# Last stage of a fused linear-attention and GLU kernel: transposes one pair ahead, numerators in one piece, and a longer wait for x tiles

## The chip, the cores and the metric

The kernel runs on one core of a Trainium2 chip. Its engines work side by side, each through its own queue of instructions in a fixed order: TensorE (PE) multiplies matrices into eight PSUM banks, VectorE (DVE) and ScalarE (ACT) can read these banks, GpSimd (POOL) works on on-chip tiles only, and SyncE (SP) starts the transfers (DMA). An instruction that waits holds up everything behind it on its own engine. The metric is the time of one execution on the device, in microseconds.

## The reference, cut to what matters

```python
xn = layernorm(x)                                   # x: 2048 x 1024, f32
q, k, v = split(xn @ wqkv)                          # 32 heads of 32
phi(t) = concat(softmax(t @ w_phi), softmax(-(t @ w_phi)))
num = phi(q) @ (phi(k).T @ v);  den = phi(q) @ sum(phi(k)) + 1e-6
s = (num / den) @ wo
h = sigmoid(xn @ w_gate) * (xn @ w_up)              # 2048 x 3584
g = silu(h @ w_down)
out = x + s * g
```

## The kernel before, in words

Every large product is one level of a Strassen-like scheme: seven products (`B11, T2, T3, B21, T1, T4, B22`) of half-size blocks, summed in PSUM and by DVE. Each f32 operand is held as a high and a low part; `split` makes them (the high part by an ACT cast, L219, the low part by a DVE subtraction, L220), and `mm3` issues three matmuls (L224, L225, L226), 128 x 128 by 128 x 512 each. So one "product" in the text below is one `mm3`, three matmul instructions, unless an operation of the scheme is meant.

The stages follow each other on PE: projections, the GLU's first layer (in two chunks of rows, c = 0 and 1), its second layer (the "down" stage, L1279 and on), and the last stage, attention output times `wo`.

Beside the products, generator tasks do the rest of the work in small steps. While chunk 0 of the GLU runs, `x_task` prepares the eight row tiles of chunk 1: it loads a tile, normalises it (L269 to L284: statistics on DVE, a square root and the scaling on ACT), writes it to DRAM in another order (`xs_d`, four DMAs, L665) and reads it back (L667). After three `yield`s, each one step of the task, two DVE transposes (L672) put it in place; in the second tile of each couple `x_sums` adds eight POOL pieces (L79). POOL also makes the sums of the GLU weights (`glu_sums`) and the gate products `pool.mul` (L79 too) that let DVE reuse the buffers of `u1` and `u2` (L1185, L1188).

The last stage runs over eight pairs of row tiles (`tp_`, L1348). A pair is seven operations of four products (28 products, 84 matmuls): B11, T2, T3, B21, T1, T4, B22. Their sums read the banks: L1370 (T2), L1376 (T3), L1383 (B21), L1386 (T1, T4, B22); T4 adds into the bank of T3 and B22 into that of T1, so B22's first product waits until T1's sum has been read. Beside a pair the operands of the next one are made: eight DVE transposes of the weighted features (`phi_transpose`, L817: for each half of the heads hb, each tile u, each q; the second for a tile starts the DMA of the next features, L810, from `f_d`), then `numerators` (16 matmuls of 64 rows, L832, which the profile lists as 32 records), four ACT copies out of their banks (L837), and `o_operands`: four POOL sums of two pieces each and seven splits.

The order in which the code calls these is only the starting point: a scheduler reorders the instructions of each engine by its own estimate, unless `tc.issue_after(i)` holds a piece back behind instruction `i` in that estimate. `attend` gives the places in a pair: transposes at the products 1 to 4 and 8 to 11, numerators at product 13. Nothing anchors them in before.

Of the kernel before, what the change touches and what calls it, by code (L numbers as in the profile page):

```python
# [17 lines left out]
P = 128  # L18
# [120 lines left out]
def hedgehog_glu_kernel(  # L139
# [82 lines left out]
    def mm3(o, a, b, first, last, **kw):  # L222

        nc.tensor.matmul(o, a[0], b[0], start=first, stop=False, **kw)  # L224
        nc.tensor.matmul(o, a[0], b[1], start=False, stop=False, **kw)  # L225
        nc.tensor.matmul(o, a[1], b[0], start=False, stop=last, **kw)  # L226

# [430 lines left out]
    def x_task(t):  # L658
        th, u = t % CTT // 4, t % 4
        xt, dst = x_load(t, 52), halves(53 + th)  # L660
        yield
        yield from norm_steps([t], [xt])
        yield
        for n in range(4):
            nc.sync.dma_start(xs_d[t - CTT, :, :, n].rearrange("q s c -> s q c"),  # L665
                              xt[n * DH:(n + 1) * DH].rearrange("s (q c) -> s q c", q=4))
        nc.sync.dma_start(xt, xs_d[t - CTT].rearrange("q s n c -> (q s) (n c)"))  # L667
        yield
        yield
        yield  # L670
        for q in range(2):
            nc.vector.transpose(dst[q].rearrange("p (k n s) -> p n k s", n=4, s=DH),  # L672
                                xt.rearrange("p (n k d) -> p n k d", n=4, d=DH)[:, :, 4 * q:4 * q + 4])
            i = {(0, 0): B11, (1, 0): B21, (1, 1): B22}.get((q, th))
            if i is not None:
                operand(1, i, u, dst[q])
        if th:
            x_sums(u, halves(53), halves(54))
# [134 lines left out]
    def phi_transpose(tp_, u, hb, q):  # L813
# [5 lines left out]
        if q:  # L819
            e_load(u)  # L820

    def numerators(tp_):

        sums = []
        for hb in range(2):
            for q in range(2):
                ps, ph = nmr.next(), units_ph[hb, q]
                kv = slots[KVB[hb]][:, q].rearrange("p (k m) -> p k m", m=P)
                for j in range(2):
                    for b in range(2):  # L830
                        bs = slice(b * 64, b * 64 + 64)
                        nc.tensor.matmul(ps[bs, j * 256:(j + 1) * 256], kv[:, 2 * j + b, bs], ph[:, 2 * j + b], start=True,  # L832
                                         stop=True, skip_group_check=True)
                sums.append((hb, q, ps))
        for hb, q, ps in sums:
            o = oraw[hb].rearrange("p u (g t) -> p u g t", t=P)
            nc.scalar.copy(o[:, :, 2 * q:2 * q + 2], ps.rearrange("p (j u t) -> p u j t", j=2, u=2))  # L837
            if q:
                o_operands(tp_, hb)
# [20 lines left out]

    def attend(tp_):

        turned = [(phi_transpose, tp_, u, hb, q) for hb in range(2) for u in range(2) for q in range(2)]
        return list(zip((1, 2, 3, 4, 8, 9, 10, 11, 13), turned + [(numerators, tp_)]))

# [198 lines left out]
    wd = [(5, lambda j=j: wd_sums(j, *(halves(47, 52) if j < WD1 else spare))) for j in range(NJ)]  # L1064
    xs = [(8, lambda t=t: x_task(t)) for t in (CTT + 4 * a + q for q in range(4) for a in range(2))]
    os = [(6, lambda k=k: o_task(k)) for k in range(4)]
# [169 lines left out]
    def evacuate(i, p):  # L1236
# [18 lines left out]
        else:  # L1255
            nc.vector.tensor_add(u1[p], u1[p], b)
            gate_out(u1[p], t, 1)
# [12 lines left out]
    for n, (i, j, cs) in enumerate(dsteps):  # L1270
        w, hs = dready[n]
        for c in cs:
            for u in range(4):
                p = 4 * c + u
                mm3(banks[p], cut(pair(hs[c]), slice(u * P, (u + 1) * P)), pair(w),
                    j == 0 and i in (B11, T2, T3, T1), j == NJ - 1, skip_group_check=True)
        wfree.append(w)
        hfree.extend(hs.values())
# [32 lines left out]
        if n == ND - NJ:  # L1311
            step(1000)
            side.extend([lambda fn=fn, a=a: behind_split(fn, *a) for _, (fn, *a) in attend(0)])
        if len(dready) == ND:
# [30 lines left out]
    for _ in range(2):  # L1345
        gx_load()
    abank = {}
    for tp_ in range(NTP):  # L1348
        nxt = attend(tp_ + 1) if tp_ + 1 < NTP else []
        n = 0  # L1350
# [5 lines left out]
        for i in range(7):  # L1356
# [4 lines left out]
            for k in range(4):  # L1361
                mm3(ps, (o[0][:, k], o[1][:, k]), pair(WO[i][k]), i in opening and k == 0, k == 3, skip_group_check=True)
                n += 1
                while nxt and nxt[0][0] <= n:
                    fn, *a = nxt.pop(0)[1]
                    fn(*a)
            if i == B11:
                nc.scalar.copy(u1, ps)
            elif i == T2:
                nc.vector.tensor_add(u1, u1, ps)  # L1370
                for r in (T4, B22) if last else ():
# [3 lines left out]
            elif i == T3:  # L1375
                nc.vector.tensor_add(u2, u1, ps)  # L1376
            else:
# [3 lines left out]
                if i == B21 or last and i != T1:  # L1381
                    y = {B21: y11, T4: y21, B22: u1}[i]
                    nc.vector.tensor_mul(y, g, ps)  # L1383
                else:
                    y = {T1: u2, T4: y21, B22: u1}[i]
                    nc.vector.tensor_add(y, u2 if i == T1 else u1, ps)  # L1386
                    eng.mul(y, y, g)
# [34 lines left out]
```

## Time and profile before

| what | value |
|---|---|
| time, median of 3 runs (lowest to highest) | 2351.07 us (2348.71 to 2352.66) |
| the profiled execution, and its span | 2350.23 us, 2348.5 us |
| PE busy | 2331.4 us, 99% of the span |
| DVE, POOL, ACT busy | 69%, 49%, 41% |
| DMA, share of 16 engines | 78% |

PE is busy nearly throughout, and its matmuls are pipelined: a row of 0.39 us does not mean that the next one starts 0.39 us later. How fast PE goes is read from the starts of consecutive matmuls. In the timeline a row gives start, duration, engine, line, operation, output and inputs, shape, count, and in brackets the idle time of the engine before it with what ended it.

### The profile page before, as it was taken

To read this page: it belongs to the slowest core of one execution; us is meant where nothing else is said; L and a number is where in the kernel's file an instruction comes from. 1 tells how busy PE (TensorE), PEld (TensorE's weight loads), DVE (VectorE), ACT (ScalarE), POOL (GpSimd) and SP (SyncE) were. 2 spreads that over 40 slices of the span, in tenths; PEclk is the share of its full clock that TensorE was granted. 3 is DMA by queue.
4 is the path that set the end of the run, shared out by engine and by line. 5 is a ranking of instruction groups with operands and counts; after the bars stand their busy time and mean duration, and the time that the engine had idled before them with its cause. 6 is when DMAs were issued, how large, how long until landed. Compare 5 with 4: busy or idle time off the path is not lost.

```text
span 2348.5 us, 32142 instructions
## 1 busy us (share of the span) xinstructions
PE 2331.4 (99%) x10644; PEld 1922.2 (82%) x10644; DVE 1624.6 (69%) x2306; ACT 957.5 (41%) x1410; POOL 1160.7 (49%) x1320
## 2 busy tenths in 40 slices
PE   9999999999999999999999999999999999999999
PEld 7888888878888888888888888888888888887777
DVE  8734788677777675466867777866666777657655
ACT  7333354445454454233435344433434333344322
POOL 3210267677686642304363544555444455623777
PEclk9999999999999999999999999999999999999999
DMA  8875566888888889858888887879777877878774
GB/s 289 298 266 188 188 213 223 278 291 300 304 309 294 281 300 362 303 186 281 270 274 284 281 270 262 287 249 344 245 235 258 276 240 232 285 261 296 241 226 162
DMA packets 265415, 624.11 MB, mean 266 GB/s; under 512 B 36896, under 2 KB 65696, under 8 KB 260640
## 3 DMA queue, kind: packets, MB, share of 16 engines
q1 hardware_dynamic: 265248, 622.05, 78.0%
q8 instruction: 84, 1.38, 0.2%
q14 instruction: 83, 0.68, 0.1%
HBM read 373.42 MB, written 248.51 MB: 265 GB/s over the span
## 4 chain that ended last, share of the span: by engine, by line
PE 90%; DMA 4%; DVE 4%; issue 1%; ACT 1%; POOL 0%; SPq 0%; DVEq 0%; ACTq 0%
PE bank L224 29%; PE bank L225 29%; PE bank L226 29%; DMA fa<-w_down 2%; PE bank L602 1%; PE bank L832 1%; PE bank L329 1%; DMA x<-xk 1%; DVE x L920 1%; DMA fc<-xs_d 0%; DVE x L220 0%; DVE w L220 0%; DMA fa<-wv 0%; DVE w L920 0%; DMA wf_d<-x 0%
## 5 line engine op out<-in xcount | busy, mean ns | idle before, releaser
L225 PE MATMUL bank<-x,w 128*128 128x512 f32 x2352 | 916.4, 390 | 0.7 <-DVE x L220 0.7
L224 PE MATMUL bank<-x,w 128*128 128x512 f32 x2352 | 906.3, 390 | 3.7 <-DVE fc L1171 2.1
L226 PE MATMUL bank<-x,w 128*128 128x512 f32 x2352 | 905.9, 389 | 0.0
L79 POOL TENSOR_TENSOR fc<-fc 128x256 f32<-128x256 f32 x488 | 427.4, 907 | 480.0 <-DMA fc<-e_d 131.6
L220 DVE TENSOR_TENSOR w<-fa,w 128x512 fp32r<-128x512 f32 (+1 forms) x436 | 397.6, 915 | 201.3 <-ACT w L219 191.6
L219 ACT CAST w<-fa 128x512 fp32r<-128x512 f32 (+1 forms) x436 | 300.3, 691 | 556.8 <-PE bank L225 354.5
L224 PEld LDWEIGHTS bank<-x,w 128*128 128x128 f32 x2352 | 441.9, 188 | 97.1 <-DVE fc L1171 2.7
L225 PEld LDWEIGHTS bank<-x,w 128*128 128x128 f32 x2352 | 442.0, 188 | 92.7 <-DVE x L220 1.9
L226 PEld LDWEIGHTS bank<-x,w 128*128 128x128 f32 x2352 | 441.8, 188 | 91.8
L224 PE MATMUL bank<-w,x 128*128 128x512 f32 x636 | 248.4, 391 | 0.3 <-DVE fc L506 0.3
L225 PE MATMUL bank<-w,x 128*128 128x512 f32 x636 | 247.9, 390 | 0.0
L226 PE MATMUL bank<-w,x 128*128 128x512 f32 x636 | 247.4, 389 | 0.0
L79 POOL TENSOR_TENSOR fb<-fa 128x256 f32<-128x256 f32 x112 | 97.9, 894 | 218.6 <-PE bank L226 110.9
L79 POOL TENSOR_TENSOR fb<-fb,fc 128x256 f32<-128x256 f32 x132 | 123.6, 957 | 121.8 <-DVE fc L1188 121.6
L79 POOL TENSOR_TENSOR fc<-fc,sa 128x256 f32<-128x256 f32 x128 | 97.0, 788 | 93.5 <-issue 85.0
L224 PEld LDWEIGHTS bank<-w,x 128*128 128x128 f32 x636 | 119.4, 188 | 26.9 <-issue 1.9
L226 PEld LDWEIGHTS bank<-w,x 128*128 128x128 f32 x636 | 119.4, 188 | 24.8
L225 PEld LDWEIGHTS bank<-w,x 128*128 128x128 f32 x636 | 119.4, 188 | 24.3
L219 ACT CAST p<-fc 128x512 fp32r<-128x512 f32 x96 | 73.0, 764 | 131.2 <-DVE fc L575 79.0
L220 DVE TENSOR_TENSOR x<-fa,x 128x512 fp32r<-128x512 f32 x112 | 93.9, 839 | 45.0 <-ACT x L219 45.0
L219 ACT CAST w<-fb 128x512 fp32r<-128x512 f32 x112 | 69.0, 617 | 118.2 <-PE bank L225 86.4
L1188 DVE TENSOR_TENSOR fc<-fc,bank 128x512 f32<-128x512 f32 x84 | 57.5, 684 | 83.5 <-PE bank L226 61.6
(208 smaller groups left out, 2824.3 us busy)
## 6 DMA issues: line engine op xcount, KB each, us to landing
ws_d<-w SPq DMA_DIRECT2D x112, 512.0 KB, 4.2
w<-ws_d SPq DMA_DIRECT2D x112, 512.0 KB, 5.2
fa<-w_gu SPq DMA_DIRECT2D x84, 512.0 KB, 4.8
fa<-h_d SPq DMA_DIRECT2D x84, 512.0 KB, 4.9
fa<-wf_d SPq DMA_DIRECT2D x32, 1024.0 KB, 6.1
h_d<-fc SPq DMA_DIRECT2D x120, 256.0 KB, 4.7
fa<-w_down SPq DMA_DIRECT2D x80, 256.0 KB, 5.2
h_d<-fb SPq DMA_DIRECT2D x76, 256.0 KB, 4.5
```

The source lines that it names most:

```text
L79: last = self.engine.tensor_tensor(o[:, s], a[:, s], b[:, s], op=op)
L219: nc.scalar.copy(o[0], src)
L220: return nc.vector.tensor_sub(o[1], src, o[0].bitcast(F32))
L224: nc.tensor.matmul(o, a[0], b[0], start=first, stop=False, **kw)
L225: nc.tensor.matmul(o, a[0], b[1], start=False, stop=False, **kw)
L226: nc.tensor.matmul(o, a[1], b[0], start=False, stop=last, **kw)
L329: nc.tensor.matmul(ps[:, gs], r[:, gs], bd[:, 4 * (n // 2) + g], start=True, stop=True)
L602: nc.tensor.matmul(kvb[g // 2][:, g % 2 * 256:g % 2 * 256 + 256], v[:, g].rearrange("p a f -> p (a f)"), ph[:, g].rearrange("p a f -> p (a ...
L832: nc.tensor.matmul(ps[bs, j * 256:(j + 1) * 256], kv[:, 2 * j + b, bs], ph[:, 2 * j + b], start=True, stop=True, skip_group_check=True)
L920: nc.vector.tensor_sub(o[1], src, o[0].bitcast(F32))
L1188: v = nc.vector.tensor_add(b, u2 if q == 3 else u1, bank)
```

## The change

Three parts. First, `x_task` takes five steps instead of three between the read-back of a tile and its transposes, so that a task has 10 steps and not 8. Second, the pieces beside a pair are placed anew: the transposes of the second half of the heads (hb = 1) of the next pair at products 1 to 4, its numerators at product 10, and the transposes of the first half (hb = 0) of the pair after that at products 17, 18, 21 and 22. Before the first pair, in the last steps of the down stage, two empty steps stand between the halves, and the first half of pair 1 follows the numerators of pair 0. Third, anchors: `last_mm` chains every product of the stage and the whole set of numerators one behind the other, so that the scheduler can't take the numerators apart, and `last_sum` puts each piece behind the latest sum of the pair on DVE.

```diff
-        nc.tensor.matmul(o, a[1], b[0], start=False, stop=last, **kw)
+        return nc.tensor.matmul(o, a[1], b[0], start=False, stop=last, **kw)
...
         nc.sync.dma_start(xt, xs_d[t - CTT].rearrange("q s n c -> (q s) (n c)"))
-        yield
-        yield
-        yield
+        for _ in range(5):
+            yield
...
+    last_mm = []
+
     def numerators(tp_):
         sums = []
+        with tc.issue_after(last_mm[0]):
             (the loops over hb, q, j, b as before, one level deeper)
+        last_mm[:] = [m.ins]
...
-    def attend(tp_):
-        turned = [(phi_transpose, tp_, u, hb, q) for hb in range(2) for u in range(2) for q in range(2)]
-        return list(zip((1, 2, 3, 4, 8, 9, 10, 11, 13), turned + [(numerators, tp_)]))
+    def turned(tp_, hb):
+        return [(phi_transpose, tp_, u, hb, q) for u in range(2) for q in range(2)]
+
+    def beside(tp_):
+        out = []
+        if tp_ + 1 < NTP:
+            out += list(zip((1, 2, 3, 4, 10), turned(tp_ + 1, 1) + [(numerators, tp_ + 1)]))
+        if tp_ + 2 < NTP:
+            out += list(zip((17, 18, 21, 22), turned(tp_ + 2, 0)))
+        return out
...
-    xs = [(8, lambda t=t: x_task(t)) for t in (CTT + 4 * a + q for q in range(4) for a in range(2))]
+    xs = [(10, lambda t=t: x_task(t)) for t in (CTT + 4 * a + q for q in range(4) for a in range(2))]
...
-            side.extend([lambda fn=fn, a=a: behind_split(fn, *a) for _, (fn, *a) in attend(0)])
+            for what in turned(0, 0) + [None] * 2 + turned(0, 1) + [(numerators, 0)] + turned(1, 0):
+                side.append((lambda fn=what[0], a=what[1:]: behind_split(fn, *a)) if what else lambda: None)
...
-    abank = {}
+    abank, last_sum = {}, [last_evac[0]]
     for tp_ in range(NTP):
-        nxt = attend(tp_ + 1) if tp_ + 1 < NTP else []
+        nxt = beside(tp_)
...
-                mm3(ps, (o[0][:, k], o[1][:, k]), pair(WO[i][k]), i in opening and k == 0, k == 3, skip_group_check=True)
+                with tc.issue_after(last_mm[0]):
+                    m = mm3(ps, (o[0][:, k], o[1][:, k]), pair(WO[i][k]), i in opening and k == 0, k == 3, skip_group_check=True)
+                last_mm[:] = [m.ins]
                 n += 1
                 while nxt and nxt[0][0] <= n:
                     fn, *a = nxt.pop(0)[1]
-                    fn(*a)
+                    with tc.issue_after(last_sum[0]):
+                        fn(*a)
```

Each of the sums L1370, L1376, L1383 and L1386 now also stores its instruction in `last_sum`.

Three places show how the instructions of an engine move. The lines of the changed kernel are some 10 to 15 higher in number: L834 is its numerators (L832 before), L816 its transposes (L817), L1385, L1391, L1398 and L1401 its sums (L1370, L1376, L1383, L1386).

On PE, in a pair of the last stage, before (`bank_102` takes B11 and B21, `bank_103` T2, `bank_104` T3 and T4, `bank_105` T1 and B22; `fb` holds the transposed features, `p` the key-value blocks). The first piece stands in B21, the second behind T4, and the last rows are the next pair's B11, one matmul of its T2, and only then this pair's B22:

```order
L226 MATMUL bank_102<-w_93,x_0_91 128x512
L832 MATMUL bank_99<-fb_14626,p_14625 64x256 x3
L832 MATMUL bank_100<-fb_14626,p_14625 64x256 x4
L832 MATMUL bank_101<-fb_14626,p_14625 64x256 x4
L224 MATMUL bank_102<-w_93,x_0_91 128x512
...
L226 MATMUL bank_104<-x_0_90,fa_16054 128x512
L832 MATMUL bank_98<-fb_14626,p_14625 64x256 x4
L832 MATMUL bank_99<-fb_14626,p_14625 64x256
L224 MATMUL bank_102<-x_1_771,fa_16054 128x512
...
L224 MATMUL bank_103<-x_0_89,x_0_91 128x512
L224 MATMUL bank_102<-w_93,x_0_91 128x512
```

and of the changed kernel, in T3, and from T4 to B22:

```order
L226 MATMUL bank_104<-x_3_15479,x_0_91 128x512
L834 MATMUL bank_98<-fb_14626,p_14625 64x256 x4
L834 MATMUL bank_99<-fb_14626,p_14625 64x256 x4
L834 MATMUL bank_100<-fb_14626,p_14625 64x256 x4
L834 MATMUL bank_101<-fb_14626,p_14625 64x256 x4
L224 MATMUL bank_104<-x_3_15479,x_0_91 128x512
...
L226 MATMUL bank_104<-x_0_90,fa_16060 128x512
L224 MATMUL bank_105<-x_2_16061,fa_16060 128x512
```

The scheduler of before took five of a set's 16 numerators ahead by 17 products and left eleven behind product 13; over the whole stage its 128 numerators stand in 18 pieces (8, 4, 4, 1, 10, 5, 1, 15, then five times 5 and 11). In the changed kernel they stand in 8 pieces of 16. Before, B22 stands 13 matmuls behind T4; now it follows T4 at once.

On DVE, in the same stage, from T3's sum of one pair to T2's sum of the next, before:

```order
L1376 TENSOR_TENSOR fc_97<-fc_97,bank_104 128x512
L817 STREAM_TRANSPOSE fb_14626<-fc_97 128x4x4x32 x2
L220 TENSOR_TENSOR x_1_611<-fc_97,x_1_611 128x512
L220 TENSOR_TENSOR fa_16054<-fc_97,fa_16054 128x512
L817 STREAM_TRANSPOSE fb_14626<-fc_97 128x4x4x32 x2
L220 TENSOR_TENSOR x_0_91<-fc_97,x_0_91 128x512
L1383 TENSOR_TENSOR fc_97<-fc_97,bank_102 128x512
L220 TENSOR_TENSOR fa_16054<-fc_97,fa_16054 128x512
L817 STREAM_TRANSPOSE fb_14626<-fc_97 128x4x4x32 x2
L220 TENSOR_TENSOR x_0_91<-fc_97,x_0_91 128x512
L1386 TENSOR_TENSOR fc_97<-fc_97,bank_105 128x512
L220 TENSOR_TENSOR x_1_611<-fc_97,x_1_611 128x512
```

and of the changed kernel, from T2's sum to T4's (`bank_103` is T2's bank, `bank_105` T1's):

```order
L1385 TENSOR_TENSOR fc_97<-fc_97,bank_103 128x512
L220 TENSOR_TENSOR x_1_611<-fc_97,x_1_611 128x512
L220 TENSOR_TENSOR fa_16060<-fc_97,fa_16060 128x512
L1391 TENSOR_TENSOR fc_97<-fc_97,bank_104 128x512
L220 TENSOR_TENSOR x_0_91<-fc_97,x_0_91 128x512
L220 TENSOR_TENSOR fa_16060<-fc_97,fa_16060 128x512
L220 TENSOR_TENSOR x_0_91<-fc_97,x_0_91 128x512
L1398 TENSOR_TENSOR fc_97<-fc_97,bank_102 128x512
L816 STREAM_TRANSPOSE fb_14626<-fc_97 128x4x4x32 x2
L220 TENSOR_TENSOR x_1_611<-fc_97,x_1_611 128x512
L220 TENSOR_TENSOR fa_16060<-fc_97,fa_16060 128x512
L1401 TENSOR_TENSOR fc_97<-fc_97,bank_105 128x512
```

Before, five of the seven splits stand ahead of T1's sum (the first L1386) and two behind it; now all seven stand ahead of it, with two transposes among them instead of six.

On POOL, beside the GLU, from the end of one unit's weight sums over the `x_sums` of the second x tile (the first `fc_97<-fc_97` rows) to the next gate product (the second or third such row, x2), before:

```order
L79 TENSOR_TENSOR fb_96<-fa_95,fb_96 128x256 x2
L79 TENSOR_TENSOR fc_97<-fc_97 128x256 x7
L79 TENSOR_TENSOR fb_96<-fa_95 128x256 x2
L79 TENSOR_TENSOR fc_97<-fc_97 128x256
L79 TENSOR_TENSOR fb_96<-fb_96,fa_95 128x256
L79 TENSOR_TENSOR fb_96<-fa_95 128x256
L79 TENSOR_TENSOR fb_96<-fb_96,fa_95 128x256
L79 TENSOR_TENSOR fb_96<-fa_95 128x256
L79 TENSOR_TENSOR fc_97<-fc_97 128x256 x2
```

and of the changed kernel:

```order
L79 TENSOR_TENSOR fb_96<-fa_95,fb_96 128x256 x2
L79 TENSOR_TENSOR fc_97<-fc_97 128x256 x6
L79 TENSOR_TENSOR fb_96<-fa_95 128x256 x2
L79 TENSOR_TENSOR fc_97<-fc_97 128x256 x2
L79 TENSOR_TENSOR fb_96<-fb_96,fa_95 128x256 x2
L79 TENSOR_TENSOR fc_97<-fc_97 128x256 x2
```

The gate product (the last row of each) now stands ahead of the two pieces `fb_96<-fa_95` of the third weight sum. The DVE transposes of that tile (L672) stay right behind T2's sum of the same unit, L1169, with two reductions of a query task (L545, L546) now in between; and on ACT the square root of the next tile, L273, moves behind four of the GLU's instructions (three casts and the copy L1167).

## Rows read from the trace of the kernel before

**Rows 1.** Busy time by stretch: us, engines' busy (instructions), PE clock, DMA share, GB/s

```profile
0.00:2348.50 2348.50, 2331.41 (x10644) 1922.23 (x10644) 1624.57 (x2306) 957.50 (x1410) 1160.72 (x1320) 1.00 0.78 266
498.80:502.30 3.50, 3.50 (x11) 2.69 (x10) 1.87 (x4) 2.19 (x3) 2.76 (x4) 0.51 1.00 236
```

**Rows 2.** Timeline of PE in a pair of the last stage

```profile
2239.95 0.39 PE L226 MATMUL bank<-w,x 128*128 128x512 f32 x1
2240.27 2.80 PE L832 MATMUL bank<-fb,p 128*64 128x256 f32 x22
...
2243.35 0.40 PE L225 MATMUL bank<-w,x 128*128 128x512 f32 x1
...
2250.43 0.39 PE L226 MATMUL bank<-x,x 128*128 128x512 f32 x1
2250.75 1.51 PE L832 MATMUL bank<-fb,p 128*64 128x256 f32 x10
...
2252.53 0.39 PE L225 MATMUL bank<-x,x 128*128 128x512 f32 x1
```

**Rows 3.** Timeline of PE, end of the down stage

```profile
2133.48 1.08 PE L832 MATMUL bank<-fb,p 128*64 128x256 f32 x8 [0.83 <-DVE fb L817]
...
2150.78 0.50 PE L225 MATMUL bank<-x,w 128*128 128x512 f32 x1 [0.53 <-DVE x L220]
...
2156.38 0.50 PE L225 MATMUL bank<-x,w 128*128 128x512 f32 x1 [0.22 <-DVE x L220]
```

**Rows 4.** Timeline of DVE, end of the down stage

```profile
2129.96 1.31 DVE L817 STREAM_TRANSPOSE fb<-fc 128x512 f32<-128x512 f32 x2 [1.88 <-DMA fc<-f_d]
```

**Rows 5.** Timeline of DVE and ACT in the pair of rows 2

```profile
2244.39 1.02 DVE L220 TENSOR_TENSOR fa<-fc,fa 128x512 fp32r<-128x512 f32 x1 [1.04 <-ACT fa L219]
...
2250.30 0.70 DVE L220 TENSOR_TENSOR x<-fc,x 128x512 fp32r<-128x512 f32 x1
2250.93 0.68 DVE L1386 TENSOR_TENSOR fc<-fc,bank 128x512 f32<-128x512 f32 x1
...
2250.49 0.62 ACT L219 CAST fa<-fc 128x512 fp32r<-128x512 f32 x1 [1.27 <-POOL fc L79]
```

**Rows 6.** Instructions by line, last stage: busy us, mean ns, idle before

```profile
L220 DVE TENSOR_TENSOR x<-fc,x 128x512 fp32r<-128x512 f32 x32 | 28.5, 894 | 9.9 <-ACT x L219 9.8
```

**Rows 7.** Timeline of PE beside the x tiles

```profile
485.91 0.39 PE L226 MATMUL bank<-x,w 128*128 128x512 f32 x1
487.76 0.47 PE L224 MATMUL bank<-x,w 128*128 128x512 f32 x1 [1.46 <-DVE fc L1188]
...
495.80 0.39 PE L226 MATMUL bank<-x,w 128*128 128x512 f32 x1
498.31 0.50 PE L224 MATMUL bank<-x,w 128*128 128x512 f32 x1 [2.12 <-DVE fc L1171]
...
498.88 0.63 PE L226 MATMUL bank<-x,w 128*128 128x512 f32 x1
...
502.29 0.39 PE L225 MATMUL bank<-x,w 128*128 128x512 f32 x1
```

**Rows 8.** Timeline of DVE beside the x tiles

```profile
471.68 1.31 DVE L672 STREAM_TRANSPOSE fc<-fc 128x512 f32<-128x512 f32 x2 [3.67 <-DMA fc<-xs_d]
...
486.92 0.69 DVE L1188 TENSOR_TENSOR fc<-fc,bank 128x512 f32<-128x512 f32 x1 [4.78 <-POOL fc L79]
```

**Rows 9.** Timeline of POOL beside the x tiles

```profile
472.47 7.28 POOL L79 TENSOR_TENSOR fc<-fc 128x256 f32<-128x256 f32 x7 [7.07 <-DVE fc L672]
...
484.78 0.74 POOL L79 TENSOR_TENSOR fb<-fa 128x256 f32<-128x256 f32 x1
485.48 1.42 POOL L79 TENSOR_TENSOR fc<-fc 128x256 f32<-128x256 f32 x2
```

**Rows 10.** Timeline of ACT beside the x tiles

```profile
489.27 0.20 ACT L273 ACTIVATE lnw<-lnw 128x1 f32<-128x1 f32 x1 [8.87 <-DVE lnw L272]
```

**Rows 11.** Issues of line L810, the feature loads of the last stage

```profile
DMA to landing us min/median/max: 3.2/4.2/9.2
```

More of the change, by code (lines that the diff above doesn't have):

```diff
@@ L820, in phi_transpose @@
             e_load(u)
+    last_mm = []
     def numerators(tp_):
         sums = []
[L825 to L834, printed above, removed]
+        with tc.issue_after(last_mm[0]):
+            for hb in range(2):
+                for q in range(2):
+                    ps, ph = nmr.next(), units_ph[hb, q]
+                    kv = slots[KVB[hb]][:, q].rearrange("p (k m) -> p k m", m=P)
+                    for j in range(2):
+                        for b in range(2):
+                            bs = slice(b * 64, b * 64 + 64)
+                            m = nc.tensor.matmul(ps[bs, j * 256:(j + 1) * 256], kv[:, 2 * j + b, bs], ph[:, 2 * j + b],
+                                                 start=True, stop=True, skip_group_check=True)
+                    sums.append((hb, q, ps))
+        last_mm[:] = [m.ins]
         for hb, q, ps in sums:
@@ L1255, in evacuate @@
         else:
-            nc.vector.tensor_add(u1[p], u1[p], b)
+            last_evac[:] = [nc.vector.tensor_add(u1[p], u1[p], b).ins]
             gate_out(u1[p], t, 1)
@@ L1274, in hedgehog_glu_kernel @@
                 p = 4 * c + u
-                mm3(banks[p], cut(pair(hs[c]), slice(u * P, (u + 1) * P)), pair(w),
+                m = mm3(banks[p], cut(pair(hs[c]), slice(u * P, (u + 1) * P)), pair(w),
                     j == 0 and i in (B11, T2, T3, T1), j == NJ - 1, skip_group_check=True)
+        last_mm[:] = [m.ins]
         wfree.append(w)
@@ L1361, in hedgehog_glu_kernel @@
             for k in range(4):
-                mm3(ps, (o[0][:, k], o[1][:, k]), pair(WO[i][k]), i in opening and k == 0, k == 3, skip_group_check=True)
+                with tc.issue_after(last_mm[0]):
+                    m = mm3(ps, (o[0][:, k], o[1][:, k]), pair(WO[i][k]), i in opening and k == 0, k == 3, skip_group_check=True)
+                last_mm[:] = [m.ins]
                 n += 1
@@ L1369, in hedgehog_glu_kernel @@
             elif i == T2:
-                nc.vector.tensor_add(u1, u1, ps)
+                last_sum[:] = [nc.vector.tensor_add(u1, u1, ps).ins]
                 for r in (T4, B22) if last else ():
@@ L1375, in hedgehog_glu_kernel @@
             elif i == T3:
-                nc.vector.tensor_add(u2, u1, ps)
+                last_sum[:] = [nc.vector.tensor_add(u2, u1, ps).ins]
             else:
@@ L1382, in hedgehog_glu_kernel @@
                     y = {B21: y11, T4: y21, B22: u1}[i]
-                    nc.vector.tensor_mul(y, g, ps)
+                    last_sum[:] = [nc.vector.tensor_mul(y, g, ps).ins]
                 else:
                     y = {T1: u2, T4: y21, B22: u1}[i]
-                    nc.vector.tensor_add(y, u2 if i == T1 else u1, ps)
+                    last_sum[:] = [nc.vector.tensor_add(y, u2 if i == T1 else u1, ps).ins]
                     eng.mul(y, y, g)
```

## The prediction

> **What bounds the kernel now.** I read the busy time by stretch first. PE is busy for 2331.41 of the 2348.50 us of the span [rows 1], so time can go only in two ways: less work on PE, or fewer of the some 17 us in which it stands idle. The second view is the timeline of PE, read by starts: between the matmuls that start at 2243.35 and 2250.43 [rows 2] there are 31 steps, so one matmul costs 7.08 / 31 = 0.228 us there, and whatever lies further apart than that is a loss, whether the row calls it idle or not. Such losses stand where the change moves things in three places: at every piece of numerators in the last stage [rows 2], at three stalls in the last steps of the down stage [rows 3], and at two stalls beside the x tiles [rows 7]. The third view is the timelines of DVE, POOL and ACT at those places; they say who was late.
>
> **Part one: the numerators in one piece.** The 22-record piece takes from the matmul before it (2239.95) to the second one behind it (2243.35) 3.40 us; the 10-record piece takes 2252.53 − 2250.43 = 2.10 us in the same measure [rows 2]. Without a piece two steps would be 2 x 0.228 = 0.46 us, so the pieces cost 2.94 and 1.64 us. Twelve records more cost 1.30 us, 0.108 each; what is left, 1.64 − 10 x 0.108 = 0.56 us, is the price of a piece whatever its length (the way into it, and the slower first matmul behind it). The number of matmuls does not change; the pieces fall from 18 to 8. 10 x 0.56 = 5.6 us come off PE itself. Nothing can hide or give this back except a new stall. Bounds: five of the ten pieces that vanish are cut like these two, the others are between one and ten matmuls long, and the price is measured on two; 4.5 to 6.5 us.
>
> **Part two: the end of the down stage.** PE waits 0.83 us for a transpose, then 0.53 and 0.22 for splits [rows 3], 1.58 us in all. All three come from DVE standing behind transposes whose features had not landed: 1.88 us idle at 2129.96 [rows 4]. The new order gives these loads two empty steps and has 12 transposes there, not 16, ahead of the split that PE needs. I book all of it, −1.6 us; bounds 0 (the last four transposes now come behind the first numerators, and could hold the same splits) and −1.6.
>
> **Part three: the new wait at B22.** In before, 13 matmuls stand between T4 and the pair's B22; the chain of anchors takes them away, so B22, which adds into T1's bank, must now find T1's sum done. And all seven splits stand ahead of that sum on DVE, five before. Let T0 be the start of a pair's numerators (2240.27 in rows 2).
> B22's own time: the block of 32 records is over, in steps of PE, at T0 + 3.08 (the way from 2240.27 to 2243.35) + 10 x 0.108 − 0.23 = 3.93. Behind it come 42 matmuls (the two last products of T3, then B21, T1, T4): 42 x 0.228 = 9.58. B22 could start at T0 + 13.5.
> T1's sum by DVE's work: the split at 2244.39 starts at T0 + 4.12 [rows 5] and moves by the ten records that now come first, 1.08, to 5.20. From it on come its own 1.02, then five splits at 0.89 [rows 6], three sums at 0.68 (T3, B21, T1) [rows 5] and two transposes, 1.31 [rows 4]: 8.8 us. Instructions of DVE overlap a little (the row of 2250.30 lasts 0.70, the next starts 0.63 later [rows 5]), ten times 0.07 off: 8.1. The sum ends at 13.3; PE goes on some 0.15 behind such an end (486.92 + 0.69 against 487.76 [rows 7, 8]): T0 + 13.5.
> T1's sum by the way over POOL and ACT: the last cast, 2250.49 [rows 5], is T0 + 10.22, with the 1.08 at 11.3; its 0.62, the split 0.89, the sum 0.68 and 0.15 make T0 + 13.6.
> So both ways end where B22 begins, with no room. I take 0.3 us a pair, for what swings: seven pairs, +2.1 us. Bounds 0, and 1.3 a pair, where each of the five splits takes 1.02 like the one of 2244.39 and nothing overlaps (5 x 0.13 + 0.7): 9.1 us.
> The Trainium skill bears on this (SBUF — State Buffer, section "Who interferes with whom"): a DVE instruction that reads two SBUF operands and a GpSimd instruction that reads SBUF shut each other out for a whole instruction. The trace agrees in part: the splits, with two such operands, take 0.89 us in the mean [rows 6], sums with one operand in PSUM 0.68 [rows 5]. Seven splits in a row beside POOL's sums would by that rule be slower than the mean, which speaks for the upper bound and the second rival.
> T4's bank needs T3's sum, which stands five DVE instructions earlier than T1's while T4 starts only 12 matmuls before B22; no wait is booked there.
>
> **Part four: the x tiles.** Two stalls and what follows: 487.76 − 485.91 − 0.23 = 1.62, then 498.31 − 495.80 − 0.23 = 2.28 [rows 7]; behind the second, PE runs at its 1.2 GHz level (granted clock 0.51 [rows 1]), and the eight matmuls from 498.88 to 502.29 take 3.41 us where 8 x 0.228 = 1.82 would do: 1.6 more. In all 5.5 us. The cause goes back to one transpose that waits for a tile: DVE idle 3.67 at 471.68 [rows 8], POOL idle for it 7.07, then seven x sums, 7.28 [rows 9]; the gate product at 485.48 comes late, DVE waits 4.78 for it [rows 8], and ACT's square root stands 8.87 us for statistics behind that [rows 10], holding casts that the second stall wants.
> In the new order the gate product stands ahead of the last two pieces of weight sums, 2 x 0.74 = 1.5 us [rows 9], so the first stall falls by about that, and ACT has four instructions less behind the square root. But the transposes stay right behind the sum that they followed, two short reductions aside: the wait of 3.67 is not visibly shortened in this couple, and seven more tiles move with other neighbours. I book 1.5 and half of the other 4.0: −3.5 us. Bounds 0 and −5.5, and +4 if the tiles, two steps later each, stall PE elsewhere (as long as these two stalls together, 3.9).
>
> **Sum.** −5.6 − 1.6 + 2.1 − 3.5 = −8.6 us. The profiled execution took 2350.23 us, so 2341.6; the median of the runs shown is 0.8 above it, so I say 2342.5.
>
> **Rivals.**
> The x stage keeps its stalls (its cause, the late tile, has the same neighbours on DVE [rows 8]; against it, the gate product does move up). Then −5.6 − 1.6 + 2.1 = −5.1: 2346.0. Chance 0.2.
> T1's sum holds B22 for the upper bound, 1.3 us a pair: +9.1 in place of +2.1, so −1.6: 2349.5. For it speaks that both ways to this sum end without room; against it, that DVE has slack elsewhere in the pair (1.04 us idle before 2244.39 [rows 5]). Chance 0.14.
> Slower: late features. The load behind the transposes of product 22 is issued when these are done, T1's sum at T0 + 13.4 and two transposes, T0 + 14.7 and, with the copy to SP's queue, about 15; its tile must be turned (1.31) before the next numerators at T0 + 84 x 0.228 + 32 x 0.108 + 0.56 = T0 + 23.2. It has 6.9 us, and takes 4.2 in the median but up to 9.2 [rows 11]. If loads between stores of results all took 9.2, six pairs would each lose 2.3: +14 − 8.6 = +5.4, 2356.5. It decides from a landing of 6.9 us on; the median speaks against it. Chance 0.06.
> Everything comes back: no wait at B22 and no stall beside the x tiles: −5.6 − 1.6 − 5.5 = −12.7, 2338.4. Chance 0.12.
> That the anchors do not hold the numerators together is excluded: the new order shows eight pieces.
>
> **How the numbers follow.** The forecast has 0.48. Its own range, half of each bound, is 2339.5 to 2345.5. The range for 8 in 10 takes in the first and the last rival and reaches to the second: 2337.5 to 2349.5. A measurement here can tell 0.2%, 4.7 us, from no change: faster means under 2346.4. The forecast (nearly all of it), the last rival and some half of the first make faster 0.67; half of the first, the second and the edge of the forecast make same 0.27; the third rival makes slower 0.06.
>
> **What would show it.** Eight pieces of L834 in PE's timeline, each with its 0.56 us; a period of a pair near 23.2 to 23.7 us. At B22's first matmul a bracket with the DVE sum of T1: none or about 0.3 us, against 1.3 for the second rival. Waits of DVE for f_d inside the pairs would show the third. At 485 to 503 us a first stall of some 0.2 us and a second of half its size without the low clock; both unchanged means the first rival. I am wrong if the stretch between 430 and 760 us takes longer than before, or if pairs take over 24 us.

## The result: 0.17% slower, and the profile after

The changed kernel took 2353.78 us in the median of 22 runs, the kernel before 2350.11 in 22 runs beside them; the ratio is 1.0017, 95% interval 1.0011 to 1.0023. One of the 22 executions of the kernel before took 6993 us and is not in the ratio. So it is some 4 us slower, where I had forecast 8.6 us faster. The profiled execution took 2354.14 us, with a span of 2352.4.

Both programs have the same 10,644 matmul records, so the starts of the n-th one in the two traces say where the time went:

| stretch (records) | before, us | after, us | difference |
|---|---|---|---|
| start of the kernel (0 to 580), same order in both | 109.16 | 111.44 | +2.3 |
| x tiles, first half (2150 to 3000) | 198.93 | 194.10 | −4.8 |
| x tiles, second half, and what follows (3000 to 4000) | 226.67 | 231.31 | +4.6 |
| end of the down stage, first pair (9600 to 9862) | 57.23 | 58.90 | +1.7 |
| the other pairs (9862 to the end) | 161.18 | 161.02 | −0.2 |

The parts between these stretches agree within 0.1 us. The first line is chance: over all traces of this study, in which nothing differs there, that stretch takes 108.1 to 111.4 us. The timeline of PE of the changed kernel, with the rows that answer to [rows 2, 3, 7]:

```profile
496.74 0.50 PE L224 MATMUL bank<-x,w 128*128 128x512 f32 x1 [0.50 <-DVE fc L1181]
501.21 0.50 PE L224 MATMUL bank<-x,w 128*128 128x512 f32 x1 [0.28 <-ACT fb L1189]
...
692.72 0.51 PE L224 MATMUL bank<-x,w 128*128 128x512 f32 x1 [0.57 <-ACT fc L1189]
...
842.03 0.50 PE L224 MATMUL bank<-w,x 128*128 128x512 f32 x1 [0.69 <-ACT fc L509]
...
2158.23 0.50 PE L225 MATMUL bank<-x,w 128*128 128x512 f32 x1 [1.66 <-DVE x L220]
...
2184.18 0.50 PE L224 MATMUL bank<-x,x 128*128 128x512 f32 x1 [0.89 <-DMA x<-wo_d]
...
2216.63 0.39 PE L226 MATMUL bank<-x,x 128*128 128x512 f32 x1
2216.95 3.67 PE L834 MATMUL bank<-fb,p 128*64 128x256 f32 x32
...
2220.89 0.40 PE L225 MATMUL bank<-x,x 128*128 128x512 f32 x1
...
2229.98 0.39 PE L226 MATMUL bank<-x,x 128*128 128x512 f32 x1
2230.81 0.50 PE L224 MATMUL bank<-x,fa 128*128 128x512 f32 x1 [0.44 <-DVE fc L1401]
```

The two stalls of [rows 7] are down to 0.50 and 0.28 us and the clock stays up, but six short waits stand between 690 and 845 us (two are shown, the first and the last) where the kernel before has none. The piece at 2216.95 costs 2220.89 − 2216.63 − 0.46 = 3.80 us, against 2.94 + 1.64 for the two of before. The last row is B22: it starts 0.83 us behind the matmul before it instead of 0.23, and its second matmul 0.34 behind instead of 0.23: 0.71 us, in each of seven pairs. What it waits for is the sum of T1 (L1401):

```profile
2228.21 0.80 DVE L220 TENSOR_TENSOR fa<-fc,fa 128x512 fp32r<-128x512 f32 x1
2229.14 1.01 DVE L220 TENSOR_TENSOR x<-fc,x 128x512 fp32r<-128x512 f32 x1
2230.08 0.68 DVE L1401 TENSOR_TENSOR fc<-fc,bank 128x512 f32<-128x512 f32 x1
```

That sum stands right behind the seventh split, whose cast ACT could start only when POOL's sum was there, in a run of fourteen sums:

```profile
2228.49 0.62 ACT L219 CAST x<-fc 128x512 fp32r<-128x512 f32 x1 [0.77 <-POOL fc L79]
```

```profile
2220.98 12.69 POOL L79 TENSOR_TENSOR fc<-fc 128x256 f32<-128x256 f32 x14 [3.91 <-DVE fa L220]
```

### The profile page after: what moved, and what is told of

It is laid out like the page before. It is cut to its first block, busy times and chain, and to the rows that moved or that the text cites. A ratio compares the mean times of both kernels' runs of the same rounds, so it can differ in the third digit from the quotient of the medians.

```text
span 2352.4 us, 32119 instructions
## 1 busy us (share of the span) xinstructions
PE 2328.5 (99%) x10644; PEld 1921.3 (82%) x10644; DVE 1627.8 (69%) x2306; ACT 959.6 (41%) x1411; POOL 1164.5 (50%) x1320
## 4 chain that ended last, share of the span: by engine, by line
PE 81%; issue 5%; DVE 5%; DMA 4%; POOL 4%; ACT 1%; SPq 0%; POOLq 0%; DVEq 0%; ACTq 0%
PE bank L224 26%; PE bank L225 26%; PE bank L226 26%; POOL fc L79 3%; PE bank L602 1%; DMA fc<-f_d 1%; PE bank L329 1%; DMA fc<-g_d 1%; POOL fb L79 1%; DMA fa<-wv 1%; DVE x L930 1%; PE bank L1006 1%; DMA fc<-xo_d 1%; DMA fc<-xs_d 0%; DVE fb L816 0%
## 5 line engine op out<-in xcount | busy, mean ns | idle before, releaser
L79 POOL TENSOR_TENSOR fb<-fb 128x256 f32<-128x256 f32 x44 | 43.7, 1013 | 148.0 <-DMA fb<-w_down 148.0
```

The costliest lines, as they stand in the source:

```text
L79: last = self.engine.tensor_tensor(o[:, s], a[:, s], b[:, s], op=op)
```

## The experiments

Each kernel was timed beside the kernel before on the same chip; "faster" and "slower" without more are against that one. The runs are spread over several chips (e1 to e4 on one, e5, e6 and e7 on a second, e8, e9 and e10 on a third, e11 and e12 on a fourth); kernels on different chips are compared by their ratios. e1 and e2 divide the change in two, and each executes in the same order as the changed kernel in its part.

**e1, the x tiles alone**, on the kernel before:

```diff
-        yield
-        yield
-        yield
+        for _ in range(5):
+            yield
...
-    xs = [(8, lambda t=t: x_task(t))
+    xs = [(10, lambda t=t: x_task(t))
```

> The kernel before with the change of the x tiles alone (five steps instead of three, ten instead of eight in a task). Theory A (the late waits are part of the change): the trace of the changed kernel has 5.5 us of stalls at 485 to 502 us shrunk to 1.1, but six short waits between 690 and 842 us that the kernel before does not have, 3.7 us in all: so 0 to 1 us faster than before, and the same six waits, each within 0.3 us, in this trace. Rival B (the six waits are chance of that execution, as the 2.3 us more in the first 100 us may be): about 4.4 us faster than before, 2345.7, and no waits at 690 to 842 us.

Ratio 0.9991 (0.9982 to 1.0000), 2347.49 us: between the two. The trace has a gain of 5.0 us in the first half of the x tiles and gives 2.8 back in the second, in two late waits (0.7 and 1.3 us) and a short one of 0.1, and not in the six that I expected. So the late waits come with the five steps, but their number and size vary from one execution to the next.

**e2, the last stage alone** (the changed kernel with the diff of e1 turned back).

> The changed kernel with the x tiles as before (three steps, eight): only the end of the down stage and the last stage are new. Theory A: numerators in one piece give 5.6 us, seven waits of B22 for the sum of T1 take 0.60 + 0.11 us each, 5.0, the first pair waits 1.9 us for operands of wo and the end of the down stage 0.9 us more than before: 2 us slower than before. Rival B: the x part is what slows the changed kernel, and this one is 3 us or more faster than before, with waits at B22 under 0.3 us.

Ratio 1.0010 (1.0001 to 1.0019), 2353.00 us, 2.1 us slower, as theory A says; six waits at B22 of 0.60 us and one of 0.65 (by starts), with 0.1 behind each.

**e3, two transposes behind the sum of T1**, on e2:

```diff
-            out += list(zip((17, 18, 21, 22), turned(tp_ + 2, 0)))
+            out += list(zip((21, 22, 25, 26), turned(tp_ + 2, 0)))
```

> As e2, but the transposes of the first half for the pair after next stand at products 21, 22, 25 and 26, so that the first two come behind the sum of T1 on DVE instead of ahead of it. Theory A1 (DVE's own work ahead of the sum holds B22): the wait falls by the 1.29 us of two transposes, so it is gone, and the kernel is 5 us faster than e2. Rival A2 (the last split ahead of the sum waits for ACT's cast and that for POOL's sums): the wait stays at 0.4 to 0.7 us a pair and the kernel is within 1.5 us of e2. Rival A3 (features late): the loads start one or two products later, DVE waits for them inside the pairs and PE for the numerators: slower than e2.

Ratio 1.0009 (1.0000 to 1.0018), 2352.40 us: like e2. Taking 1.3 us of work out of DVE's way changed nothing, because DVE then waited for casts: 0.69 us ahead of the last split but one, which took 1.25 us, and 0.14 ahead of the last, 1.00 us (the first row below holds both):

```profile
2201.40 2.40 DVE L220 TENSOR_TENSOR x<-fc,x 128x512 fp32r<-128x512 f32 x2 [0.69 <-ACT x L219]
2203.72 0.68 DVE L1402 TENSOR_TENSOR fc<-fc,bank 128x512 f32<-128x512 f32 x1
```

```profile
2204.45 0.50 PE L224 MATMUL bank<-x,x 128*128 128x512 f32 x1 [0.43 <-DVE fc L1402]
```

So A1 falls here: with two transposes less ahead of it, the sum of T1 ends where it did, 13.8 us behind the start of the numerators, since the last splits wait for their casts. The seventh pair of e2 says the same: it has no transposes there either, and waits its 0.60 us. A3 came true at one set of numerators, where PE waited 0.66 us at 2264.09 for a transpose whose features landed late.

**e4, B22 free of the chain**, on e2 (its four products carry `last_sum[0]` instead of `last_mm[0]` and do not enter `last_mm`):

```diff
-                with tc.issue_after(last_mm[0]):
+                with tc.issue_after(last_mm[0] if i != B22 else last_sum[0]):
...
-                last_mm[:] = [m.ins]
+                if i != B22:
+                    last_mm[:] = [m.ins]
```

> As e2, but B22 is not tied to the chain of products, so that it stands behind the next pair's B11, 14 matmuls later, as before; the numerators stay in eight pieces. Theory A: the wait of B22 goes, 5 us faster than e2, 3 us faster than before. Rival: another wait takes its place, since the sums of T1 and B22 and with them the next pair's first bank move together: within 1.5 us of e2.

Ratio 0.9980 (0.9971 to 0.9989), 2345.25 us: 7.7 us faster than e2 and 5.7 than before, where I had expected 5 and 3. B22 stands 14 matmuls later, none of the seven waits is left, and the pairs behind the first take 157.00 us (161.18 before). More than the seven waits goes in e4: PE's waits for `wo_d` in the first pair, 2.6 us in e2 with what follows each, fall to 0.5 as well.

**e5, numerators at product 8**, on e2:

```diff
-            out += list(zip((1, 2, 3, 4, 10), turned(tp_ + 1, 1) + [(numerators, tp_ + 1)]))
+            out += list(zip((1, 2, 3, 4, 8), turned(tp_ + 1, 1) + [(numerators, tp_ + 1)]))
```

> As e2 (x tiles as before, B22 tied behind T4), but a set of numerators stands at product 8 of a pair instead of 10, so that it and all that follows from it starts 6 matmuls, 1.4 us, earlier against B22. All seven splits still stand ahead of the sum of T1. Theory A2 (the way from the numerators over ACT's copies, POOL's sums, ACT's cast and the last split to the sum of T1 is what ends at B22): the seven waits of 0.60 us go, and the kernel is 5 us faster than e2. Rival (something that does not start at the numerators holds the sum, such as the sum of T1's own bank or a transfer): the waits stay and the kernel is within 1 us of e2. Rival (the transposes are late for product 8): the waits at B22 go, and waits of PE at the numerators for DVE come in their place, 0.3 us or more a pair.

Ratio 1.0012 (1.0003 to 1.0020), 2352.91 us. I had this wrong: the wait is longer, not gone, 0.74 us by starts in five pairs (0.39 in one, and none in the seventh).

```profile
2229.05 0.51 PE L224 MATMUL bank<-x,fa 128*128 128x512 f32 x1 [0.58 <-DVE fc L1402]
```

Counted from the start of the numerators, the sum of T1 ends at 15.3 us in these five pairs, against 13.8 in e2 and, but for one pair, in e3. Splits moved ahead of T3's and B21's sums, and the last split stands behind B21's sum and two transposes: in the pair of this row its own cast was over at 2225.85, and it started at 2227.49. The seventh pair has no such transposes, since there is no pair after next; there the sum ends at 13.85 us and B22 does not wait. A2, in the form that the way from the numerators alone ends at B22, falls with this.

**e8, the sum of T1 ahead of the last two splits**, on e2: `o_operand` for T1 and T4 becomes `late_operands(tp_)`, called at product 21, behind the sum of T1.

```diff
-        o_operand(tp_, T1, b11)
-        o_operand(tp_, T4, b21)
...
+        if tp_ + 1 < NTP:
+            out.insert(7 if tp_ + 2 < NTP else 5, (21, (late_operands, tp_ + 1)))
...
             (at the entry, (late_operands, 0) also follows (numerators, 0))
```

> As e2 (x tiles as before, B22 tied behind T4), but the last two operands of a set (T1's and T4's for the next pair) are split behind the sum of T1: on DVE five splits stand ahead of that sum, as before the change, and two behind it. Theory D (the sum of T1 itself has long been possible, and stands in DVE's queue behind splits whose casts wait for POOL's sums): the seven waits of 0.60 us at B22 go, 5 us faster than e2, about 2348. Rival A1 (DVE's own work ahead, transposes and sums included): the wait falls by the two splits, 1.9 us, and goes as well, but then e3, which took two transposes (1.3 us) away, should have lost it too; so D and A1 differ only in e3. Rival (what ends the wait is T1's bank itself, the matmuls or the sum's own time): the wait stays at 0.6 us and the kernel is within 1 us of e2.

Ratio 0.9995 (0.9986 to 1.0004), 2348.55 us. By the ratios it is 3.5 us faster than e2, by the traces 4.5 us in the pairs behind the first (156.50 against 161.00), with B22 tied as in the change. Its trace has no wait at B22: the sum ends at 2228.26, 12.9 us behind the start of the numerators, and the last two splits come behind it.

```profile
2227.59 0.67 DVE L1407 TENSOR_TENSOR fc<-fc,bank 128x512 f32<-128x512 f32 x1
2228.18 1.83 DVE L220 TENSOR_TENSOR x<-fc,x 128x512 fp32r<-128x512 f32 x2
```

```profile
2228.62 0.39 PE L224 MATMUL bank<-x,fa 128*128 128x512 f32 x1
```

e3, e5 and e8 together: what sets the wait is the place of the sum in DVE's queue, behind two splits which it does not need. In the changed kernel and in e3 the last of these wait for casts and so for POOL's sums; in e5 the last one stands behind two transposes.

**e6, the entry**, on e4: the four transposes of pair 1 that stood behind the first numerators move into pair 0.

```diff
-            for what in turned(0, 0) + [None] * 2 + turned(0, 1) + [(numerators, 0)] + turned(1, 0):
+            for what in turned(0, 0) + [None] * 2 + turned(0, 1) + [(numerators, 0)]:
...
+            if tp_ == 0:
+                out += list(zip((1, 2, 3, 4, 5, 6, 7, 8, 13), turned(1, 0) + turned(1, 1) + [(numerators, 1)]))
+            else:
+                (the five pieces as in the change)
```

> As e4 (x tiles as before, B22 free of the chain), but the four transposes for pair 1 that the change put behind the first numerators, still in the down stage, are moved into pair 0 (eight transposes at products 1 to 8, numerators at 13 in this pair alone). Theory C (these four hold the splits that the last down products wait for, 1.83 us at one matmul in all four traces with the new entry, and part of 0.5 to 0.8 us at the one before): 1.8 to 2.5 us faster than e4, the 1.83 us gone. Rival (the splits are late by the two empty steps and by the w_down loads, wherever the transposes stand): the wait of 1.83 us stays, no difference from e4; or it moves into pair 0.

Ratio 0.9976 (0.9966 to 0.9986), 2345.01 us. The wait of 1.83 us fell to 0.64, by as much as two transposes take, and did not go as I had said. By the trace the end of the down stage (records 9600 to 9760) is 1.9 us shorter than in e4, 36.47 against 38.35; but the changed kernel's own trace has 36.52 there, and by the times e4 and e6 can't be told apart. So that the entry gains by this is read from one wait and not shown by the time.

**e10, the entry without empty steps**, on e6:

```diff
-            for what in turned(0, 0) + [None] * 2 + turned(0, 1) + [(numerators, 0)]:
+            for what in turned(0, 0) + turned(0, 1) + [(numerators, 0)]:
```

> e6 without the two empty steps between the halves of the first transposes. Theory C2 (the empty steps push the second half against the numerators, which wait 0.66 us for a transpose, and against the splits): 0.5 to 1.5 us faster than e6. Rival (they do what they are for: without them DVE waits for features that have not landed, as before): 0.5 to 1.5 us slower than e6. Rival: the same.

Ratio 0.9975 (0.9964 to 0.9987), 2343.95 us. In the trace the end of the down stage takes 33.94 us, against 36.47 in e6 and 35.29 before, and the waits for splits are gone; against e6 the times overlap. PE's order there is that of before again: the first set of numerators stands in the same three pieces (8, 4 and 4 matmuls), at the same records. So e10, and with it e11 and e12 (35.24 and 34.21 us there), has part two of the change all but undone, and gains mostly by the later pairs (156.47 us).

**e7, the change with B22 free**, and **e9**: the diff of e1 on e4 and on e6. So e7 differs from the changed kernel in one thing, the diff of e4.

> The changed kernel with one thing undone: B22 is not tied to the chain of products (e4 with the x tiles of the change). Theory A (the tie of B22 is the cause of the changed kernel's loss, and the x part gains by itself): the 5.7 us of e4 and the 2.2 of e1 add up, 7.9 us faster than before, 2343. Rival (the x part gives nothing here, its result in e1 was chance): like e4, 5.7 us faster than before. Rival (B22 was only part of it): under 3 us faster.

> e6 with the x tiles of the change: all three parts together (B22 free of the chain, the four transposes of pair 1 moved into pair 0, five steps in the x tiles). If the parts add up: 5.5 us of e6 and 2.2 of e1, so 7.7 us faster than before, and the fastest of all. Theory S (beside the x tiles a split of DVE can be shut out for as long as POOL runs without a pause, as the one of 7.78 us in e7; this happens in some executions of a kernel with the new x tiles): the single times fall in two groups some 7 us apart, most in the lower. Rival: the late group of e7 was chance, all times within 4 us.

e7: ratio 0.9985 (0.9975 to 0.9995), median 2344.63; e9: 0.9984 (0.9974 to 0.9995), 2346.33. Both are faster than before, so that taking one anchor away turns the change's sign; but the x part adds nothing to e4 and e6, against both of my sums. Set beside their twins with three steps, five steps cost 0.07% in the changed kernel (against e2), 0.05% in e7 (against e4) and 0.08% in e9 (against e6); only e1 gained, 0.09%. Each of these is within the noise, but the gain of e1 and the loss of e2 do not add up to the changed kernel, and the x part's share of its loss stays open to some 2 us. The times spread: e7 has eight within 2342.2 to 2346.2 and four within 2348.5 to 2353.2, e9 seven within 2342.6 to 2346.8 and four within 2349.5 to 2351.5, so not all within 4 us as the rival said; the means of the groups lie 7.3 and 6.5 us apart. The profiled execution of e7 is one of the late ones (2351.82 us), and its timelines of DVE, POOL and PE show a split of 0.7 us that lasted 7.78:

```profile
488.88 7.78 DVE L220 TENSOR_TENSOR w<-fa,w 128x512 fp32r<-128x512 f32 x1
496.58 0.68 DVE L220 TENSOR_TENSOR w<-fb,w 128x512 fp32r<-128x512 f32 x1
```

```profile
487.74 2.84 POOL L79 TENSOR_TENSOR fb<-fb,fc 128x256 f32<-128x256 f32 x4
490.54 1.42 POOL L79 TENSOR_TENSOR fc<-fc,fb 128x256 f32<-128x256 f32 x2
491.92 1.42 POOL L79 TENSOR_TENSOR fb<-fb,fc 128x256 f32<-128x256 f32 x2
493.30 2.81 POOL L79 TENSOR_TENSOR fc<-fb,fc 128x256 f32<-128x256 f32 x4
```

```profile
500.08 0.79 PE L224 MATMUL bank<-x,w 128*128 128x512 f32 x1 [4.37 <-DVE fc L1181]
```

POOL ran these twelve sums without a pause at 0.71 us each; the split ended 0.55 us behind the last. The trace of e9, from one of its faster executions, has no such split. In the first of the late waits of the changed kernel another thing stands in the way, on ACT: the scaling of an x tile (L284), a table load and an exponential, back to back, while a cast waits (the split behind it idled DVE 1.82 us, and PE waited at 692.72).

```profile
686.64 1.24 ACT L284 ACTIVATE fc<-fc,lnw 128x1024 f32<-128x1024 f32 x1 [3.52 <-DVE lnw L281]
687.90 1.28 ACT L552 ACT_TABLE_LOAD   x1
689.19 1.06 ACT L552 ACTIVATE p<-p 128x1024 f32<-128x1024 f32 x1
690.16 0.60 ACT L219 CAST w<-fb 128x512 fp32r<-128x512 f32 x1
```

**e11 and e12, four and seven steps** for the x tiles, on e10 (e12; e11 has 4 and 9):

```diff
-        yield
-        yield
-        yield
+        for _ in range(7):
+            yield
...
-    xs = [(8, lambda t=t: x_task(t))
+    xs = [(12, lambda t=t: x_task(t))
```

> e10 (x tiles as before) with four steps between the read-back of an x tile and its transposes instead of three, nine in a task. If what the x part gives at 485 to 502 us (DVE's wait for the tile: 3.67 us before, 1.3 to 1.5 with five steps) is a matter of how long the tile has to land, four steps give part of the 4.4 us there. If what it takes at 690 to 842 us (1.9 to 5.6 us in the traces with five steps, none with three) comes from where the steps of the x tasks fall against the GLU's units, four steps change it by an amount of their own. Sum by theory: between 4 us faster and 2 us slower than e10. Theory X0 (the two parts cancel whatever the number of steps): within 1.5 us of e10.

> e10 with seven steps instead of three, twelve in a task. The tile has landed before its transposes come (wait under 0.5 us), so the stalls at 485 to 502 us are under 1 us. Theory X0: later waits between 580 and 850 us take as much or more, within 2 us of e10 or slower. Rival: the late waits belong to five steps only, and this kernel is 4 us faster than e10 and the fastest of all.

e11: ratio 0.9952 (0.9939 to 0.9964), 2339.13 us; e12: 0.9947 (0.9934 to 0.9961), 2338.36 us, 12 us faster than before. These two are the fastest of all and can't be told apart. In e12 the transposes find their tile landed, but for one wait of 0.87 us at 448.74 which holds up nothing on PE, and PE is busy for the whole stretch from 485 to 850 us: 27 records more than in the changed kernel (the first fence is the changed kernel, the second e12, columns as in [rows 1]). e11 has two waits there, 1.2 us at 493.95 and 0.8 at 799.85.

```profile
485.00:850.00 365.00, 361.53 (x1585) 296.57 (x1584) 271.95 (x399) 181.04 (x251) 261.99 (x296) 1.00 0.84 293
```

```profile
485.00:850.00 365.00, 365.00 (x1612) 302.20 (x1612) 272.64 (x401) 186.96 (x260) 260.53 (x296) 1.00 0.86 302
```

```profile
477.71 1.30 DVE L671 STREAM_TRANSPOSE fc<-fc 128x512 f32<-128x512 f32 x2
```

So the late waits do not come of waiting longer as such: none in the traces with three steps or seven, 0.8 us in the one with four, 2.1 to 4.4 us in the four with five, not counting what follows each. My theory X0 falls. Why five steps meet the GLU's units so badly was not tried.

## Why the prediction was wrong, step by step

- **Part one, numerators** (−5.6): the gain was right and a little small, the rule behind it not. Two pieces become one for 0.78 us, not 0.56 (2.94 + 1.64 − 3.80), in five of the sets; e8, where nothing waits at B22, shows the gain undiluted: the pairs behind the first take 156.50 us against 161.18. My 0.108 us a record, fitted to two pieces, would make 32 records 0.2 us dearer than 30. In the two traces they take the same: of before, the piece of 30 records, 15 matmuls, lasts 3.67 us, as the whole set of 16 does in the changed kernel, and both cost 3.80. The smallest piece, one matmul, costs 2180.56 − 2179.33 − 0.46 = 0.77:

```profile
2192.01 3.67 PE L832 MATMUL bank<-fb,p 128*64 128x256 f32 x30
```

```profile
2179.33 0.39 PE L226 MATMUL bank<-x,x 128*128 128x512 f32 x1
2179.65 0.65 PE L832 MATMUL bank<-fb,p 128*64 128x256 f32 x2
...
2180.56 0.39 PE L225 MATMUL bank<-x,x 128*128 128x512 f32 x1
```

Pieces of 1, 4, 5, 8, 10, 11, 15 and 16 matmuls cost 0.77, 1.22, 1.64, 2.08, 2.51, 2.94, 3.80 and 3.80 us in the two traces. All fit an estimate of 0.35 us a piece and 0.43 for every two matmuls, where an odd one left over costs as much as two. Seven of the eight sets of before are cut at an odd place, so by this estimate the ten pieces are worth 10 x 0.35 + 7 x 0.43 = 6.5 us, the upper end of my bounds.

- **Part three, B22** (+2.1): the mechanism was right and mis-sized: 7 x 0.71 = 5.0 us. The sum of T1 ended at T0 + 13.8 in the changed kernel (2230.76 − 2216.95), where I had 13.3 and 13.5, since the last cast started at T0 + 11.5 and not 11.3 and the split behind it took 1.01 us and not 0.89; and B22 could have started at T0 + 13.3, not 13.5. (T3's sum stands nine places ahead of T1's in DVE's queue, not five; there no wait came, as I had said.) I took 0.3 "for what swings" between two ways that both ended there without room, and left out the slow second matmul behind every wait. The second rival had the right place; its 1.3 us a pair was 0.6 too high, my 0.3 was 0.4 too low. e4 and e8 take the wait away by two different edits; with e4's the change turns faster than before, its x part included (e7).
- **Part two, the entry** (−1.6): wrong sign. I saw that the last four transposes "could hold the same splits" and put the bound at 0; the wait at 2158.23, 1.66 us, is in large part that: the split which it waits for stands behind two of them on DVE, and in e6, without them, the wait is shorter by what they take. My bounds held no loss here, and the seven traces with the new entry take 36.5 to 38.4 us for the end of the down stage, the two with the old one 34.2 and 35.3.

```profile
2156.32 1.29 DVE L816 STREAM_TRANSPOSE fb<-fc 128x512 f32<-128x512 f32 x2
2157.54 0.64 DVE L220 TENSOR_TENSOR x<-fa,x 128x512 fp32r<-128x512 f32 x1
```

- **T4's and T1's operands in the first pair**: not in my sum at all. Four loads of `wo_d`, blocks of `wo`, stand on SP behind waits for transfers of the gate's results and were issued 4.0 us later than before; PE waits 0.89 and 0.49 us for them, 1.9 us with what follows. In e4, where B22 comes later, 0.5 us of this is left; in e8, with B22 tied, it stays. Why the loads go out later was not tried. The first row is the kernel before, the second the changed one:

```profile
2172.63 1.74 SPq L805 DMA_DIRECT2D x<-wo_d  x4
```

```profile
2176.68 1.74 SPq L804 DMA_DIRECT2D x<-wo_d  x4
```

- **Part four, the x tiles** (−3.5): right at the place that I looked at, −4.8, and wrong in the stage: +4.6 later, the bound of "+4 if the tiles stall PE elsewhere", which I gave no rival and no chance. I had worked out one couple out of the four that the eight tiles make. At that place, too, more happened than I had said: the transposes' wait for the tile, which I took as "not visibly shortened", fell from 3.67 to 1.53 us.

```profile
472.55 1.30 DVE L671 STREAM_TRANSPOSE fc<-fc 128x512 f32<-128x512 f32 x2 [1.53 <-DMA fc<-xs_d]
```

By stretch of the table the errors add up so: x tiles 3.3 us (−3.5 against −0.2); end of the down stage and first pair 5.8 (−1.6, five vanishing pieces at 0.56 and one wait of 0.3 make −4.1, against +1.7); later pairs 0.8 (−2.8 + 1.8 = −1.0, against −0.2, since the pieces gave more than I took); start 2.3, which is chance. These 12.2 us lead from −8.6 to the +3.6 at which the last matmul stands. The slower side had one rival in my account, the late features, which did not come about: in the pairs PE waits for no feature. What decided were four losses: the wait at B22 and the late waits of the x stage, whose bounds I had and did not count on the slower side; the entry, whose place I had, with a bound of 0; and the loads of `wo_d`, which I had not seen. Of my two signs of being wrong only the first pair gave one, with 25.6 us from its set of numerators to the next; the other pairs took 23.6 us, and the stretch from 430 to 760 us was shorter than before, since five of the six late waits come behind it.

## What to carry to other kernels

A chain that orders one engine also decides whom it waits for: before tying an instruction, look what stands ahead of its releaser in the other engine's queue, and move that (e8) or leave the instruction loose (e4). Where two ways to an event end just when it is needed, give the wait a chance of its own on the slower side (0.3 us a pair was booked, 0.71 measured, and the upper bound of 1.3 would have missed by more), and give every moved group of instructions a loss as well as a gain. A number of steps that shifts a periodic task against another one (five) can be worse than others on both sides of it (four, seven), so a gain is to be read over the whole stage and not at the stall that one looked at.

## What the runs showed of the hardware

In the whole trace of the changed kernel, the 288 splits of 128x512 with no POOL sum beside them took 0.68 us each, the longest 0.69; the 420 with one beside them took 0.97 in the mean and up to 1.29 (0.92 in the mean of the group shown, of the last stage). POOL pays as well: of the fourteen sums at 2220.98, six took 1.18 to 1.23 us, the others 0.73 to 0.75. Tiny operations show the same. In the changed kernel, with POOL's sums running, a 128x1 reciprocal, with one operand, takes 0.15 us, and the 128x1 operations with two operands behind it 0.50 and 0.66. In e7, where POOL stood still at that place, these two take 0.16 (the last fence).

```profile
L220 DVE TENSOR_TENSOR x<-fc,x 128x512 fp32r<-128x512 f32 x33 | 30.1, 923 | 25.5 <-ACT x L219 24.3
```

```profile
494.01 0.15 DVE L275 RECIPROCAL lnw<-lnw 128x1 f32<-128x1 f32 x1
494.19 0.50 DVE L277 TENSOR_TENSOR lnw<-lnw 128x1 f32<-128x1 f32 x1
494.73 0.66 DVE L278 TENSOR_TENSOR lnw<-lnw 128x1 f32<-128x1 f32 x1
```

```profile
498.70 0.16 DVE L277 TENSOR_TENSOR lnw<-lnw 128x1 f32<-128x1 f32 x1
498.89 0.16 DVE L278 TENSOR_TENSOR lnw<-lnw 128x1 f32<-128x1 f32 x1
```

The Trainium skill's rule (SBUF — State Buffer, section "Who interferes with whom") that a DVE instruction with two SBUF operands and a GpSimd instruction which reads SBUF exclude each other agrees with these rows. The same page (section "Summary: rules for kernel authors") says that the second to issue is blocked until the first finishes; the row of 7.78 us goes further, past some ten POOL instructions in a row. No other split of 128x512 in the fourteen traces took over 2.3 us. That POOL's run held it is read from the ends of the rows; it was not tried by itself, and a run without a pause is not enough: in the changed kernel POOL ran on from 484 to 502 us, and the splits there took 0.71 to 1.25 us. Why one execution of a kernel falls into this and another doesn't stays open: the late times of e7 and e9 fit it, but only one of them was profiled.
